# One pool of 4 KB slots, a rescaled rational step, and |h| added by an accumulating DMA

## The chip, the cores and the metric

The kernel runs on one core of a Trainium2 chip. The metric is the device time of one launch in microseconds (us). The core has TensorE (PE) for matmuls, VectorE (DVE), ScalarE (ACT) and GpSimd (POOL) for elementwise work, and SyncE (SP), which here only issues transfers (DMAs). All of them work in parallel and wait for each other through semaphores. Each of ACT, DVE, PE and POOL executes its own instructions strictly in the order in which the program was written out.

## The reference

Three layers over 12480 tokens of 128 channels, float32:

```python
a2k = softmax(scale * agents @ k.T); agent_v = a2k @ v            # 49 agents
x1  = softmax(scale * q @ agents.T) @ agent_v                     # (12480, 128)
h   = x1 @ w_in;   x2 = (h * sigmoid(h)) @ w_out                  # w_in (128, 2048)
h   = x2 @ w2_in                                                  # w2_in (128, 2048)
P   = a[0] + a[1]*h + a[2]*h**2 + a[3]*h**3
Q   = 1 + |b[0]|*|h| + |b[1]|*h**2
out = (P / (Q + 1e-06)) @ w2_out                                  # (12480, 128)
```

The four weight matrices come as float64 and go to the chip as their bits; the kernel turns them into float32 itself.

## The kernel before, in words

At the start SP queues 43 loads (`LOADS`: 13 of k, 13 of v, 16 pieces of 512 KB of the weights, the first of q). k is transposed on PE (step KT), scored against the agents (KS), exponentiated (EX), transposed back (ET) and multiplied with v (AV); the result goes into the weight of the first layer (F0 to F4, V0 to V2). A piece of the weights goes through C0 and C2 on DVE, C1 on ACT, C3 on POOL, and for w2_in C4 (ACT) and C5 (POOL) as well.

Then come 25 groups g of 512 tokens (the last has 192). For each group 8 pairs p of 128-wide hidden chunks run through these steps; h is a 128x1024 tile in PSUM, of which there are three slots:

- M1 (PE, L537 and L538): h of the first layer; S1 (ACT, L544): silu; M2 (PE, L551): the sum into one PSUM bank, x2. XS (DVE, L564 and L565) splits x2 into a high and a low part.
- M3 (PE, L574 to L576): h of the second layer. U (DVE L585 for four pairs, ACT L583 for the other four): a3*h + a2. W1 and W2 (DVE, L610, L614): two more Horner steps. AB (ACT, L592): |h|. N and Q (POOL, L598, L606): the denominator without its 1. An h slot is free again when AB and W2 have read it.
- L and R (ACT, L619, L622): Ln and then the sigmoid of its negative, which is the reciprocal of the denominator. They run over two pairs at a time (128x2048). Ln, sigmoid, silu and exp need different tables, so the Ln and sigmoid of a group come as a batch, with a table load (1.28 us) at each change.
- G2 (DVE, L626): the last Horner step times the reciprocal; M4 (PE, L635): the sum into one PSUM bank, ot. O1 (ACT, L647) copies it out, O2 (PE, L655) transposes it into the same bank, O3 (ACT, L661) copies that out, and SP stores it. The next group's M4 needs the bank back, that is O3.

Every second group a batch of q is transposed, scored and normalised (QT, QTc, QS, QV, QX, QM, QE, QN, QB, QBc, QBl) to give the input of M1 for two groups; QTc (L459) and QBc (L516) are ACT copies.

The order of all of this is not found at run time. `scheduled()` simulates the steps with the costs in `COST` and the numbers in `PLACE`, which set the preference of a step over others on its engine, and the program is written out in that order. Tiles in SBUF come from one ring for each kind: s 5, z 13, m 2, y 6 (8 KB each), and so on.

Of the kernel before, what the change touches and what calls it, by code (L numbers as in the profile page):

```python
# [100 lines left out]


def group_steps(groups, pairs, part=1.0):
# [60 lines left out]
    for job in range(16):  # L164
# [7 lines left out]
        split = job // 4 == 2  # L172
        after = [("C2", job, 0)] + [("KS", batches - 1, 0)] * (job >= 12)
        stage(3, after, [("w2", ("w2", job))] * split, [("cb", job)])
        if split:
            stage(4, [("C3", job, 0)], [], [("w2", job)])
            stage(5, [("C4", job, 0)], [], [("w2", job)])
    conv += [("V2", n, 0) for n in range(4)]
    for g in range(groups):
        b = g // 2  # L180
        for p in range(pairs):
            first = [("V2", p // 2, 0)] if g == 0 else []
            add("M1", g, p, [("QBl", b, 0)] + first, [("h", ("h1", g, p))], [("xt", b)])
            add("S1", g, p, [("M1", g, p)], [("s", ("s", g, p))], [("h1", g, p)])
            first = [("C3", 4 + p // 2, 0)] if g == 0 else []
            add("M2", g, p, [("S1", g, p)] + [("M2", g, p - 1)] * (p > 0) + first, [("x2", ("x2", g))] if p == 0 else [], [("x2", g), ("s", g, p)])
# [810 lines left out]
```

## Time and profile before

| | |
|---|---|
| median of 3 runs | 1265.34 us (1263.23 to 1265.42) |
| profiled execution, first to last instruction (span) | 1261.5 us |
| median run less that span | 3.8 us |
| busy share of the span | PE 98%, ACT 85%, DVE 80%, POOL 61% |
| mean granted clock of PE | 0.996 |

No separate time was recorded for the profiled execution, so its time is taken as its span and the 3.8 us around it. Busy time of PE is the union of its matmuls, whose ends are modelled; a gap between two matmuls is a real wait. The rows say what ended the idle time before an instruction, in square brackets.

### The profile page before, as it was taken

To read this page: it belongs to the slowest core of one execution; us is meant where nothing else is said; L and a number is where in the kernel's file an instruction comes from. 1 tells how busy PE (TensorE), PEld (TensorE's weight loads), DVE (VectorE), ACT (ScalarE), POOL (GpSimd) and SP (SyncE) were. 2 spreads that over 40 slices of the span, in tenths; PEclk is the share of its full clock that TensorE was granted. 3 is DMA by queue.
4 is the path that set the end of the run, shared out by engine and by line. 5 is a ranking of instruction groups with operands and counts; after the bars stand their busy time and mean duration, and the time that the engine had idled before them with its cause. 6 is when DMAs were issued, how large, how long until landed. Compare 5 with 4: busy or idle time off the path is not lost.

```text
span 1261.5 us, 12078 instructions
## 1 busy us (share of the span) xinstructions
PE 1235.0 (98%) x4393; PEld 740.7 (59%) x4393; DVE 1003.4 (80%) x960; ACT 1076.0 (85%) x997; POOL 764.2 (61%) x434
## 2 busy tenths in 40 slices
PE   9899899999999999999999999999999999999987
PEld 5656465556556556556566565565555565555654
DVE  4977887888868869869869869769769769769895
ACT  7677988988988988988988978978978979978896
POOL 2248667666566656656655755755755755755863
PEclk9999999999999999999999999999999999999999
DMA  9820000000000000000000000000000000000000
GB/s 343 303 78 1 1 17 9 8 17 9 9 17 9 8 18 9 9 17 9 9 17 9 9 17 9 9 17 9 1 25 9 1 12 9 1 8 9 9 1 20
DMA packets 14675, 34.75 MB, mean 28 GB/s; under 512 B 1575, under 2 KB 5720, under 8 KB 14616
## 3 DMA queue, kind: packets, MB, share of 16 engines
q1 hardware_dynamic: 14616, 33.98, 7.4%
q8 instruction: 35, 0.57, 0.2%
q14 instruction: 24, 0.20, 0.0%
HBM read 27.59 MB, written 6.39 MB: 27 GB/s over the span
## 4 chain that ended last, share of the span: by engine, by line
PE 86%; DVE 6%; ACT 4%; DMA 2%; issue 1%; POOL 0%; SPq 0%; POOLq 0%; ACTq 0%; DVEq 0%
PE x L551 25%; PE ot L635 23%; PE h L537 7%; PE h L574 7%; PE h L538 7%; PE h L576 7%; PE h L575 7%; DVE z L610 2%; DVE z L614 1%; DVE z L585 1%; PE h L468 1%; PE h L451 1%; DMA kv<-in_k_dram 1%; PE ot L655 1%; DVE z L626 1%
## 5 line engine op out<-in xcount | busy, mean ns | idle before, releaser
L598 POOL TENSOR_SCALAR y<-m,bab 128x1024 f32<-128x1024 f32 (+1 forms) x200 | 265.4, 1329 | 409.8 <-ACT m L592 402.9
L606 POOL TENSOR_TENSOR y<-y,m 128x1024 f32<-128x1024 f32 (+1 forms) x200 | 469.0, 2357 | 7.5
L551 PE MATMUL x<-s,wo 128*128 128x512 f32 (+1 forms) x800 | 358.9, 584 | 3.1 <-ACT s L544 2.8
L635 PE MATMUL ot<-z,w2o 128*128 128x512 f32 x768 | 349.8, 596 | 6.8 <-DVE z L626 4.6
L610 DVE TENSOR_TENSOR z<-z,h 128x1024 f32<-128x1024 f32 (+1 forms) x200 | 237.8, 1191 | 141.2 <-ACT z L583 134.1
L626 DVE SCALAR_TENSOR_TENSOR z<-z,a_sb,y 128x1024 f32<-128x1024 f32 (+1 forms) x200 | 264.6, 1372 | 4.7 <-ACT y L622 4.7
L592 ACT ACTIVATE m<-h 128x1024 f32<-128x1024 f32 (+1 forms) x200 | 197.1, 1000 | 81.2 <-PE h L576 72.9
L614 DVE SCALAR_TENSOR_TENSOR z<-z,a_sb,h 128x1024 f32<-128x1024 f32 (+1 forms) x200 | 249.9, 1252 | 5.0 <-ACT m L592 0.5
L544 ACT ACTIVATE s<-h 128x1024 f32<-128x1024 f32 (+1 forms) x200 | 193.3, 1005 | 59.5 <-PE h L538 59.1
L635 PEld LDWEIGHTS ot<-z,w2o 128*128 128x128 f32 x768 | 143.6, 190 | 162.2 <-issue 145.1
L551 PEld LDWEIGHTS x<-s,wo 128*128 128x128 f32 x800 | 147.7, 190 | 138.5 <-issue 127.0
L574 PE MATMUL h<-xh,w2l 128*128 128x512 f32 (+1 forms) x400 | 190.9, 477 | 1.6 <-DVE z L614 1.2
L619 ACT ACTIVATE y<-y,eps 128x2048 f32<-128x2048 f32 (+1 forms) x100 | 191.4, 1957 | 0.8 <-POOL y L606 0.5
L537 PE MATMUL h<-xt,w1a 128*128 128x512 f32 (+1 forms) x400 | 185.9, 466 | 0.8 <-DVE z L614 0.7
L622 ACT ACTIVATE y<-y 128x2048 f32<-128x2048 f32 (+1 forms) x100 | 185.0, 1878 | 0.3
L576 PE MATMUL h<-xh,w2h 128*128 128x512 f32 (+1 forms) x400 | 155.9, 390 | 0.0
L575 PE MATMUL h<-xl,w2h 128*128 128x512 f32 (+1 forms) x400 | 155.3, 388 | 0.0
L538 PE MATMUL h<-xt,w1b 128*128 128x512 f32 (+1 forms) x400 | 155.1, 389 | 0.0
L585 DVE TENSOR_SCALAR z<-h,a_sb 128x1024 f32<-128x1024 f32 (+1 forms) x100 | 130.8, 1312 | 5.7 <-PE h L576 3.8
L583 ACT ACTIVATE z<-h,a_sb 128x1024 f32<-128x1024 f32 (+1 forms) x100 | 118.3, 1184 | 5.5 <-PE ot L635 3.5
L537 PEld LDWEIGHTS h<-xt,w1a 128*128 128x128 f32 x400 | 75.6, 189 | 44.1 <-issue 16.0
L574 PEld LDWEIGHTS h<-xh,w2l 128*128 128x128 f32 x400 | 75.9, 190 | 36.7 <-issue 20.0
(108 smaller groups left out, 855.1 us busy)
## 6 DMA issues: line engine op xcount, KB each, us to landing
q<-in_q_dram SPq DMA_DIRECT2D x12, 512.0 KB, 3.3
out_dram<-ob SPq DMA_DIRECT2D x24, 256.0 KB, 2.0
raw<-in_moe_w_in_dram SPq DMA_DIRECT2D x8, 512.0 KB, 4.9
raw<-in_moe_w_out_dram SPq DMA_DIRECT2D x8, 512.0 KB, 7.5
s<-in_k_dram SPq DMA_DIRECT2D x7, 512.0 KB, 7.4
kv<-in_v_dram SPq DMA_DIRECT2D x7, 512.0 KB, 7.7
kv<-in_k_dram SPq DMA_DIRECT2D x5, 512.0 KB, 10.3
s<-in_v_dram SPq DMA_DIRECT2D x5, 512.0 KB, 8.0
```

The lines of the kernel that those rows point to most:

```text
L537: nc.tensor.matmul(h[:, c, :w], w1a[:, f], xt, start=True, stop=False)
L538: nc.tensor.matmul(h[:, c, :w], w1b[:, f], xt, start=False, stop=True)
L551: nc.tensor.matmul(x2_t[i][:, : cols(i)], wo[:, 2 * p + c, :], s[:, c, : cols(i)], start=(p == 0 and c == 0), stop=(p == NP - 1 and c == 1),)
L574: nc.tensor.matmul(h[:, c, :w], w2l[:, f], xh_t[i], start=True, stop=False)
L575: nc.tensor.matmul(h[:, c, :w], w2h[:, f], xl_t[i], start=False, stop=False)
L576: nc.tensor.matmul(h[:, c, :w], w2h[:, f], xh_t[i], start=False, stop=True)
L598: nc.gpsimd.tensor_scalar(out=y_t[i, p // 2][:, p % 2], in0=m_t[i, p], scalar1=bab[:, 1:2], scalar2=bab[:, 0:1], op0=ALU.mult, op1=ALU.add,)
L606: eng.tensor_mul(out=y, in0=y, in1=m_t.pop((i, p)))
L610: nc.vector.tensor_mul(out=z, in0=z, in1=h)
L614: nc.vector.scalar_tensor_tensor(out=z, in0=z, scalar=a_sb[:, 1:2], in1=h, op0=ALU.add, op1=ALU.mult)
L626: nc.vector.scalar_tensor_tensor(out=z, in0=z, scalar=a_sb[:, 0:1], in1=r, op0=ALU.add, op1=ALU.mult)
L635: nc.tensor.matmul(ot_t[i][:, : cols(i)], w2o[:, 2 * p + c, :], z[:, c, :], start=(p == 0 and c == 0), stop=(p == NP - 1 and c == 1),)
```

## The change

- Tiles of the groups no longer come from a ring for each kind. `NF = 35` slots of 4 KB (tag `f0` to `f34`) serve s, xh and xl, z, m, y, o, q and qT alike; a step takes the slot that the planner finds free first. 20 of them lie in memory that holds k, v, raw weights and conversion tiles at the start. Before, z, m and y lay in a pool that was opened when the whole start was over.
- x2 is scaled by B0 = |b[0]| in XS (now tensor_scalar and scalar_tensor_tensor on DVE). With h' = |b[0]|*h the denominator is 1 + |h'| + kap*h'^2, with one coefficient.
- SQ (ACT, new): y = (ROOT*h')^2 = kap*h'^2, in one ACT instruction of each pair. W1 becomes y + COEF[2]*h' (DVE, scalar_tensor_tensor), and U is gone.
- Y (new): |h'| is added onto y by a DMA that POOL issues (`accum_op=ALU.add`), 512 KB of m into 512 KB of y for each pair. N and Q on POOL are gone.
- L and R run on one pair (128x1024) at a time, and a batch starts when all 8 pairs' adds are planned as done (`READY_Y = 8`).
- O1, O3, QTc and QBc go from ACT to DVE (`COPY = 'DDDD'`); O1 also multiplies by LAST.
- CF (new): 33 DVE instructions on a 128x1 column or two and 2 on ACT work out the new coefficients once, after V2.
- `LOADS` is in another order, and nearly all of `PLACE` has other numbers. `SPLIT` is empty, so the steps SH and SL and the split M2 in the diff are never made; M1 to M4 and O2 are the matmuls they were.

```diff
-LOADS = "kk0kkkkk1kkkvkk2q4kvvvvvv><vvv56vv37?v;=:98"
+LOADS = 'kk51kkkkk20kkkvkk43vkqvvvvvv8v;?vv6vv9>7<=:'
...
-READY_Y = 4
+READY_Y = 8
...
+    add("CF", 0, 0, [("V2", 3, 0)], at=-3 + PLACE["CF"][0])
...
+            add("AB", g, p, after + then("AB", g, p), [("f", m)], [h, m], cost=ABS_COST[ABS[p]])
+            if POLY[p] == "S":
+                add("SQ", g, p, after, take_y, [h, y], cost=POLY_COST[POLY[p]])
+                add("W1", g, p, [("SQ", g, p)], [("f", z)], [h, z, y])
+                add("Y", g, p, [("W1", g, p), ("AB", g, p)], [], [m, y], cost=MAG_COST[MAG[p]])
...
+    def t_f(slot, dtype=F32, shape=None):
+        pool = work if slot < NKV + NRAW + NCA + NCB else late
+        return pool.tile(shape or [P, 2, GW], dtype, tag=f"f{slot}", name=f"f{slot}", bufs=1)
...
-        nc.vector.tensor_copy(xh, ps[:, :w])
-        nc.vector.tensor_sub(out=xl, in0=ps[:, :w], in1=xh.bitcast(F32))
+        nc.vector.tensor_scalar_mul(out=xh, in0=ps[:, :w], scalar1=B0)
+        nc.vector.scalar_tensor_tensor(
+            out=xl, in0=ps[:, :w], scalar=B0, in1=xh.bitcast(F32), op0=ALU.mult, op1=ALU.subtract
+        )
...
+    def SQ(i, p, slot):
+        y = part_of(y_t, i, p, slot)
+        nc.scalar.activation(y, h2_t[i, p][:, :, : cols(i)], AF.Square, scale=ROOT)
...
+            nc.vector.scalar_tensor_tensor(
+                out=part_of(z_t, i, p, slot), in0=h, scalar=COEF[2], in1=y_t[i, p],
+                op0=ALU.mult, op1=ALU.add,
+            )
...
-            out=y_t[i, p // 2][:, p % 2], in0=m_t[i, p],
-            scalar1=bab[:, 1:2], scalar2=bab[:, 0:1], op0=ALU.mult, op1=ALU.add,
...
+        if MAG[p] == "G":
+            nc.gpsimd.dma_start(out=y, in_=m, accum_op=ALU.add)
...
-    def L(i, h):
-        nc.scalar.activation(y_t[i, h], y_t[i, h], AF.Ln, bias=eps)
+    def L(i, p):
+        nc.scalar.activation(y_t[i, p], y_t[i, p], AF.Ln, bias=eps)
...
-        nc.scalar.copy(o[:, : cols(i)], ot_t.pop(i)[:, : cols(i)])
+            nc.vector.tensor_scalar_mul(out=o[:, 0, : cols(i)], in0=ps, scalar1=LAST)
...
-        nc.scalar.copy(ob, os_t.pop((i, 2))[:n, :].rearrange("p (j c) -> p j c", c=C))
+        (nc.scalar.copy if COPY[3] == "A" else nc.vector.tensor_copy)(ob, ps)
```

Three places show what the new order does. The first is ACT where the first silu stands, at the start of group 0. Before (L929 is V1, L731 and L733 are C1, L544 is S1):

```order
L929 CAST w1a<-h 128x512 x2
L731 ACTIVATE sb<-ec 128x512
L733 ACTIVATE mf<-ma 128x512
L544 ACT_TABLE_LOAD
L544 ACTIVATE s<-h 128x1024 x3
```

And now, on the same engine at the same place (L1110 is V1, L994 and L1009 are CF's two instructions, L621 is S1):

```order
L1110 CAST w1a<-h 128x512
L994 ACTIVATE cf<-b_sb 128x2
L1009 ACTIVATE cf<-a_sb 128x4
L621 ACT_TABLE_LOAD
L621 ACTIVATE f_831<-h 128x1024
L621 ACTIVATE f_834<-h 128x1024
L621 ACTIVATE f_841<-h 128x1024
```

The first silu stands behind CF's second instruction, which writes a column that CF's first DVE instructions read, and so waits for them.

The second place is ACT in a group in the middle, where the Ln batch begins. Before, the Ln (L619) of two pairs each, with |h| (L592) and U (L583) between them:

```order
L592 ACTIVATE m<-h 128x1024 [waits PE_49,Activation_49,Pool_49]
L619 ACT_TABLE_LOAD
L619 ACTIVATE y<-y,eps 128x2048
L583 ACTIVATE z<-h,a_sb 128x1024 [waits DVE_49,PE_49]
L592 ACTIVATE m<-h 128x1024 [waits PE_49,Activation_49,Pool_49]
L619 ACTIVATE y<-y,eps 128x2048
```

And now (L711 is |h|, L687 is SQ, L742 is Ln, L550 is QV; the tile f_4351 is the y that the SQ ahead of the table load wrote, DMASW the semaphores of POOL's DMAs):

```order
L711 ACTIVATE f_4349<-h 128x1024 [waits DVE_49,PE_49]
L687 ACTIVATE f_4351<-h,cf 128x1024 [waits DMASW6_49,Activation_49]
L742 ACT_TABLE_LOAD
L742 ACTIVATE f_4159<-f_4159,eps 128x1024
L742 ACTIVATE f_4153<-f_4153,eps 128x1024
L742 ACTIVATE f_4226<-f_4226,eps 128x1024
L742 ACTIVATE f_4175<-f_4175,eps 128x1024
L550 COPY f_4366<-h 128x512 [waits DVE_49,PE_49,Activation_49]
L742 ACTIVATE f_4224<-f_4224,eps 128x1024 [waits DMASW3_49]
L742 ACTIVATE f_4278<-f_4278,eps 128x1024
L742 ACTIVATE f_4351<-f_4351,eps 128x1024 [waits DMASW7_49]
```

The group's last square is right ahead of the batch, and the seventh Ln waits for the DMA that adds onto its result. In the next group |h| of a pair stands in place of QV, one Ln further down, and the Ln that waits is the seventh again.

The third place is the end, where group 22's sum is copied out while group 24's M3 and group 23's sigmoids run. Before, on ACT (L622 sigmoid, L647 O1, L661 O3):

```order
L622 ACTIVATE y<-y 128x2048
L592 ACTIVATE m<-h 128x2x192 x2
L622 ACTIVATE y<-y 128x2048
L647 COPY oT<-ot 128x512
L583 ACTIVATE z<-h,a_sb 128x2x192
L622 ACTIVATE y<-y 128x2048
L661 COPY ob<-ot 128x512
L622 ACTIVATE y<-y 128x2048
```

And now the same copies on DVE (L737 W2, L774 O1, L749 G2, L787 O3):

```order
L737 SCALAR_TENSOR_TENSOR f_7312<-f_7312,cf,h 128x2x192
L737 SCALAR_TENSOR_TENSOR f_7305<-f_7305,cf,h 128x2x192
L774 TENSOR_SCALAR f_7319<-ot,cf 128x512
L749 SCALAR_TENSOR_TENSOR f_7159<-f_7159,cf,f_7121 128x1024
L787 COPY f_7319<-ot 128x512
L749 SCALAR_TENSOR_TENSOR f_7153<-f_7153,cf,f_7143 128x1024
```

O1 and O3 have moved from a queue with sigmoids of 2048 columns to one with Horner steps of 1024 and 384.

## Rows read from the trace of the kernel before


**Rows 1.** Windows: us, busy of each engine (instructions), granted clock, DMA share, GB/s.

```profile
0.00:30.00 30.00, 28.29 (x169) 17.95 (x169) 13.56 (x26) 21.43 (x31) 6.32 (x16) 1.00 0.91 342
...
170.00:1170.00 1000.00, 998.65 (x3292) 590.09 (x3291) 802.26 (x705) 873.88 (x754) 620.94 (x336) 1.00 0.03 11
```

**Rows 2.** Chain of waits: start, us, engine, line, two M4 stretches 14 groups apart.

```profile
416.79 6.87 PE ot L635 x16
...
1087.35 6.87 PE ot L635 x16
```

**Rows 3.** Waits of PE from 65 to 170: us in total, times, longest.

```profile
PE ot L635 <- DVE z L626: 3.2, 1, 3.2
PE x L551 <- ACT s L544: 2.8, 2, 1.9
```

**Rows 4.** The same from 1200 to the end.

```profile
PE ot L655 <- ACT oT L647: 2.2, 2, 1.8
PE ot L635 <- ACT ob L661: 2.2, 1, 2.2
PE ot L635 <- DVE z L626: 1.4, 1, 1.4
PE h L574 <- DVE z L614: 0.9, 2, 0.7
```

**Rows 5.** Timeline of PE: start, us, idle before and its releaser.

```profile
64.91 0.80 PE L537 MATMUL h<-xt,w1a 128*128 128x512 f32 x1
...
155.33 3.22 PE L551 MATMUL x<-s,wo 128*128 128x512 f32 x4 [1.91 <-ACT s L544]
...
1233.58 2.86 PE L635 MATMUL ot<-z,w2o 128*128 128x512 f32 x4 [2.19 <-ACT ob L661]
...
1257.33 0.62 PE L655 MATMUL ot<-ident,oT 128*48 128x128 f32 x4 [0.46 <-ACT oT L647]
```

**Rows 6.** Groups by line from 170 to 1170: count, busy us, mean ns, idle before.

```profile
L626 DVE SCALAR_TENSOR_TENSOR z<-z,a_sb,y 128x1024 f32<-128x1024 f32 x168 | 225.1, 1390 | 0.0
...
L614 DVE SCALAR_TENSOR_TENSOR z<-z,a_sb,h 128x1024 f32<-128x1024 f32 x168 | 214.4, 1278 | 3.9
L610 DVE TENSOR_TENSOR z<-z,h 128x1024 f32<-128x1024 f32 x167 | 203.2, 1218 | 125.8 <-ACT z L583 118.9 <-ACT m L592 5.9
L592 ACT ACTIVATE m<-h 128x1024 f32<-128x1024 f32 x168 | 169.1, 1021 | 70.8 <-PE h L576 63.8 <-DVE z L585 5.1 <-POOL y L606 1.4
L619 ACT ACTIVATE y<-y,eps 128x2048 f32<-128x2048 f32 x84 | 164.4, 2000 | 0.3
...
L585 DVE TENSOR_SCALAR z<-h,a_sb 128x1024 f32<-128x1024 f32 x84 | 112.2, 1339 | 3.6 <-PE h L576 2.7 <-ACT m L592 0.9
L583 ACT ACTIVATE z<-h,a_sb 128x1024 f32<-128x1024 f32 x83 | 100.0, 1205 | 0.4 <-PE ot L635 0.3
...
L619 ACT ACT_TABLE_LOAD x21 | 26.9, 1283 | 0.4
...
L564 DVE CAST xh<-x 128x512 fp32r<-128x512 f32 x21 | 14.5, 691 | 57.4 <-PE x L551 57.4
...
L661 ACT COPY ob<-ot 128x512 f32<-128x512 f32 x21 | 12.4, 592 | 0.3 <-PE ot L655 0.3
```

**Rows 7.** DMA issues of the page: count, KB each, median us to landing.

```profile
q<-in_q_dram SPq DMA_DIRECT2D x12, 512.0 KB, 3.3
out_dram<-ob SPq DMA_DIRECT2D x24, 256.0 KB, 2.0
```

**Rows 8.** Timeline of POOL: one instruction by itself, and one beside DVE's L626.

```profile
100.47 1.19 POOL L598 TENSOR_SCALAR y<-m,bab 128x1024 f32<-128x1024 f32 x1 [2.73 <-ACT m L592]
...
157.21 3.30 POOL L598 TENSOR_SCALAR y<-m,bab 128x1024 f32<-128x1024 f32 x1 [1.09 <-ACT m L592]
```

**Rows 9.** Timeline of SP ahead of the last v load.

```profile
48.18 5.97 SPq L703 DMA_DIRECT2D raw<-in_moe_w_out_dram  x2
```

**Rows 10.** Timeline of DVE, an instruction on one column.

```profile
35.10 0.15 DVE L859 TENSOR_TENSOR mx<-ot,mx 128x1 f32<-128x1 f32 x1
```

More of the change, by code (lines that the diff above doesn't have):

```diff
@@ L112, in add @@
             at += PLACE.get(name + ">", (0.0,))[0] * (g > groups - 3)
-        eng, c = cost or COST[name]
+        eng, c = cost or (COPY_COST[name][COPY[list(COPY_COST).index(name)]] if name in COPY_COST else COST[name])
         if name in BATCH and g == groups // 2:
@@ L182, in group_steps @@
             first = [("V2", p // 2, 0)] if g == 0 else []
[L183 to L186, printed above, removed]
-        add("XS", g, 0, [("M2", g, p) for p in range(pairs)], [("xh", ("xh", g))], [("x2", g)])
+            add("M1", g, p, [("QBl", b, 0)] + then("M1", g, p) + first + [("XS", g - 1, 0)] * (g > 0 and p > 2), [("h", ("h1", g, p))], [("xt", b)])
@@ L188, in group_steps @@
+            add("M2", g, p, [after] + [("M2", g, ORDER[at - 1])] * (at > 0) + first, x2, [("x2", g)] + uses, cost=cost)
+        add("XS", g, 0, [("M2", g, p) for p in range(pairs)] + [("CF", 0, 0)] * (g == 0), [("f", ("xh", g))], [("x2", g)])
         for p in range(pairs):
[L189 removed]
+            h, z, y = ("h2", g, p), ("z", g, p), ("y", g, p)
             first = [("C5", 8 + p // 2, 0)] if g == 0 else []
[L191 removed]
@@ L209, in group_steps @@
+        add("O1", g, 0, [("M4", g, p) for p in range(pairs)], [("f", ("o", g))], [("ot", g)])
+        add("O2", g, 0, [("O1", g, 0)], [("ot", ("o2", g))], [("o", g)])
+        add("O3", g, 0, [("O2", g, 0)], [], [("o2", g), ("o", g)])
+        add("OD", g, 0, [("O3", g, 0)], [], [("o", g)])
     for b in range(batches):
-        chain = ("QT", "QTc", "QS", "QV", "QX", "QM", "QE", "QN", "QB", "QBc", "QBl")
+        chain = ("LQ",) * (b > 0) + ("QT", "QTc", "QS", "QV", "QX", "QM", "QE", "QN", "QB", "QBc", "QBl")
@@ L221, in group_steps @@
             add(
-                name, b, 0, [(chain[i - 1], b, 0)] if i else [("M1", 2 * b - 2, 0)] if b else [land["q", 0]], [takes[name]] if name in takes else [],
+                name, b, 0, [(chain[i - 1], b, 0)] if i else [("M1", 2 * b - 2, 0)] if b else [land["q", 0]], [takes[name]] if name in takes and (b or name != "QTc") else [],
                 uses.get(name, []), at=(2 * b if b else -2) + PLACE[name][0],
@@ L241, in scheduled @@
     free = {tag: [0.0] * n for tag, n in bufs.items()}
+    free["f"] = [None] * NF
+    held_by = [(slots, set(steps), steps) for slots, steps in group_steps.freed]
     taken = {tag: 0 for tag in bufs}
@@ L270, in may_start @@
         name, g, p = k
+        kind = name + MAG[p] if name == "Y" else name
         eng, _, _, takes, _, _ = ops[k]
@@ L273, in may_start @@
         for tag, _ in takes:
-            held = free[tag] if tag == "h" else [free[tag][taken[tag] % bufs[tag]]]
+            held = free[tag] if tag in "hf" else [free[tag][taken[tag] % bufs[tag]]]
             open_ = [x for x in held if x is not None]
@@ L282, in may_start @@
                     return None
-                done = sum(all(("Q", g, 2 * h + i) in end for i in (0, 1)) for h in range(4))
+                done = sum((done_y(h), g, h) in end for h in range(8))
                 if batch is None and (p or done < READY_Y):
@@ L287, in may_start @@
                 return None
-        if name == "R" and n_ln.get(g, 0) < 4:
+        if name == "R" and n_ln.get(g, 0) < 8:
             return None
-        if name in SHARED:
-            for e, x in seen.get((SHARED[name], g, p), {}).items():
+        if kind in SHARED:
+            for e, x in seen.get((SHARED[kind], g, p), {}).items():
                 if e != eng:
                     t = max(t, x + TELL[e].get(eng, 0.1))
-        if name in PORT:
+        if kind in PORT and eng in port:
             t = max(t, port["POOL" if eng == "DVE" else "DVE"])
@@ L307, in scheduled @@
         name, g, p = k
+        kind = name + MAG[p] if name == "Y" else name
         eng, cost, _, takes, uses, _ = ops[k]
@@ L310, in scheduled @@
         idle[eng], end[k] = t + cost, t + cost + TAIL[eng]
-        if name in PORT:
+        if kind in PORT and eng in port:
             port[eng] = max(port[eng], t + cost)
-        if name in SHARED:
-            seen.setdefault((SHARED[name], g, p), {})[eng] = end[k]
+        if kind in SHARED:
+            seen.setdefault((SHARED[kind], g, p), {})[eng] = end[k]
         slot = None
         for tag, what in takes:
-            if tag == "h":
+            if tag in "hf":
                 i = slot = min(
-                    (i for i, x in enumerate(free["h"]) if x is not None), key=lambda i: free["h"][i]
+                    (i for i, x in enumerate(free[tag]) if x is not None), key=lambda i: free[tag][i]
                 )
@@ L336, in scheduled @@
                 n_sig[g] = n_sig.get(g, 0) + 1
-                batch = None if n_sig[g] == 4 else batch
+                batch = None if n_sig[g] == 8 else batch
+        for slots, left, steps in held_by:
+            if k in left:
+                left.remove(k)
+                if not left:
+                    for i in slots:
+                        free["f"][i] = max(end[x] for x in steps)
         out.append((name, g, p, slot))
@@ L952, in attention_silu_rational_kernel @@
     for name, g, p, slot in scheduled(NG, NP, REST / GW):
-        if late is None and name in ("AB", "U"):
+        if late is None and slot is not None and slot >= NKV + NRAW + NCA + NCB:
             pre.close()
```

380 lines of the change are left out of this document (257 added, 123 removed), and 69 rows, old and new, of tables (COST, PLACE).

## The prediction

> **What bounds the kernel now.** I read the windows first. From 170 to 1170 us PE is busy for 998.65 of 1000 us at the full granted clock, ACT for 873.88, DVE for 802.26 and POOL for 620.94 [rows 1]: the matmuls set the pace, and the other three fit under them. The chain of waits shows that pace: the same M4 stretch stands at 416.79 and, 14 groups later, at 1087.35 [rows 2], which is 670.56 / 14 = 47.9 us a group. As batches of q come every second group, a period is two groups, 95.8 us.
>
> The order shows the same matmuls as before, so the pace can't get shorter. What can be won is the loss of PE outside the steady stretch. The first M1 starts at 64.91 and the last O2 ends at 1257.33 + 0.62 = 1257.95 [rows 5], 1193.0 us later. 24 whole groups are 24 x 47.9 = 1149.6. Group 24 has 192 of 512 columns; its matmuls take somewhat more than that share, and I put it at 0.43 of a group, 20.6 us (an estimate). That leaves 1193.0 - 1149.6 - 20.6 = 22.8 us of loss. The waits of PE name two thirds of it: 3.2 + 2.8 = 6.0 us at the start [rows 3] and 2.2 + 2.2 + 1.4 + 0.9 = 6.7 us at the end [rows 4]. Behind two of them four M2 or M4 matmuls take 3.22 and 2.86 us [rows 5]; 128x512 matmuls of that kind stand with 6.87 / 16 = 0.43 us each in [rows 2], so 1.7 for four. Each of the two waits thus costs another 1.1 to 1.5 us in slower matmuls at once, and about 2 (an estimate) with those behind them. So about 8 us lie at the start and 8.5 at the end. Removing all of it gives 1249 at best.
>
> **The steady stretch, engine by engine.** Sums for 1000 us, by [rows 6] unless said.
>
> ACT loses the four U, 100.0 us, and the four copies: O3 is 12.4 by its row, and O1, QTc and QBc are taken like it, some 47 together. It gains a square of 1024 columns for each of 168 pairs. The trace has no square; the nearest rows are |h| with 1021 ns and U with 1205 ns, the same shape out of PSUM, so 171 to 202 us, and I take 186. L and R on halves cost nothing to 39 us: 2000 ns for 2048 columns is 1.0 us for 1024 without a fixed part, and |h| with its 1021 ns bounds the fixed part at little. So ACT stands at 873.9 - 100 - 47 + 186 + 20 = 933 (898 to 954), still below 998.65.
>
> DVE loses the other four U, 112.2, and gains the four copies. The nearest DVE row is XS with 691 ns for 512 columns: 42 x 0.69 = 29 for O1 and O3, some 27 for QTc and QBc. W1 becomes an instruction like W2, 1278 for 1218 ns, +10. G2 may keep its 1390 ns or fall to the 1278 of W2, 0 to -19. DVE: 802 - 112 + 56 + 10 - 10 = 746. CF is not in this stretch.
>
> POOL's 621 us go. In its place stands one issue for each pair; its engine is free for it.
>
> So no engine comes up to PE. I laid the printed order of one period end to end with these durations: PE stays without a gap, its h slots come free 0.6 to 1.7 us before they are wanted. I cost the steady stretch at 0, covered by these margins.
>
> **The new wait.** The seventh Ln waits for the add onto the last square of its group. Between the end of that square and this Ln stand a table load of 1.28, six Ln of 1.0 to 1.1 and one QV or |h| of 0.6 (as L661) to 1.0 us [rows 6], 7.9 to 8.9 us. W1, which reads y before the add, takes 1.28 us and a hop first, about 1.4. So 6.5 us are left for the issue and the transfer, and with 1.3 to 1.7 us of slack behind it (by the same laying out) a late add costs nothing up to about 8 us. The trace has no accumulating DMA. From below: a 512 KB load takes 3.3 us from issue to landing, 256 KB 2.0 [rows 7], so 1.3 us for 256 KB more. From above: the add reads its 512 KB of target as well, 2 x 1.3 more, 5.9 us. Issuing by software on POOL has no row; one SP issue lies below it. I take about 5 with the issue, nearer the lower end, for that row includes the read and the write of 512 KB. At 5 the seventh Ln waits for nothing. Queued behind a late Ln would be the eight sigmoids, the next silus (h slots, so M1) and through them G2 and M4.
>
> **The start.** The last v load moves from the 38th to the 37th place, with one piece fewer of the weights before it. Ahead of it SP stood 5.97 us for the raw slots of two weight pieces [rows 9], so up to that can be won. Against it the last k load has two pieces of 512 KB more ahead of it, 1 MB at 342 GB/s [rows 1], 3 us. As k's chain and v's both must end before the first M1, I take 0 (-3 to +2). CF is 33 instructions on a column at 0.15 us [rows 10], 5.0 us of DVE after V2, and the first silu waits for the first few of them, about 0.7. The rest lies beside M1 and M2 of group 0, before the first W1; if that cover is gone it costs 5. The waits of [rows 3] don't go: the first batch of Ln now needs all eight pairs, while the first M4 waits for G2 as before. I take +1 for the whole start (-3 to +6).
>
> **The end.** The two longest waits are for O1 and O3 on ACT [rows 4], each behind a sigmoid of 2048 columns (about as long as an Ln, 2.0 us [rows 6]). On DVE a copy now waits behind a Horner step of 1.28, and DVE has no U. Laid out with the row durations about 4 us of the 8.5 stay: O1, O2 and O3 still follow each other, and PE has little else to do by then. Gain 4.5 (-8 to +2).
>
> **The sum.** The profiled execution has a span of 1261.5 and 3.8 us around it, together the median of 1265.3. Start +1, steady 0, end -4.5: 1258.0 for the span, **1261.8** with what lies around it; I say 1262.
>
> **Rivals.** *The add comes late, on the seventh Ln of each group.* This ends on the other side. POOL has to write the transfer's list itself. A POOL instruction that takes 1.19 us by itself took 3.30 while DVE ran G2 [rows 8]: beside G2, which reads two tiles of SBUF, POOL was held for 2.1 us. The Trainium skill warns of just this kind of DMA (SBUF — State Buffer, 🎯 Summary: rules for kernel authors): one that POOL issues can starve for its descriptors beside some DVE instructions, and SP or ACT should issue it instead. The trace has no such DMA, and the page names DVE's two-port modes for it, not two SBUF inputs. In this kernel the price by rows is 5.9 + 0.4 + 2.1 = 8.4 us if POOL is held once and each byte of the target counts, and 10.5 if it is held twice. Beyond 8 us every group pays: 24 x 0.4 = 10 us, 24 x 2.5 = 60 us. 1270 to 1325. For it speaks that squares come every 6.0 us (47.9 / 8) and the add reads and writes 5.2 us worth of bytes by the slope; against it, that around the batch DVE has the last Horner steps, with one tile of SBUF and one of PSUM, and G2 comes after the sigmoids.
>
> *The start gets later.* CF's 5 us fall on the path, as the first Horner steps wait behind the weights' conversions on DVE, and the two k pieces' 3 us with it: +5 to +8 with the tail's gain halved, 1268 to 1273. For it: the first M4 already waits 3.2 us for DVE [rows 3]. Against it: M1 and M2 of group 0 fill PE for long before that M4.
>
> *Nothing to be seen.* The tail's gain is eaten by +3 to +5 at the start, or O1 and O3 wait behind Horner steps that themselves wait for h. 1263 to 1268.
>
> *More is won.* Without U and without POOL's 620.94 / 168 = 3.7 us for each pair [rows 1] the first group's G2 comes earlier and the 3.2 us wait goes too: -6 more, under 1256.
>
> **Chances.** The forecast 0.43, between 1256 and 1262.8; more won 0.07; nothing to be seen 0.22; a late add 0.16; a later start 0.12. A measurement of this kernel tells 0.2%, 2.5 us, from no change: faster under 1262.8, slower over 1267.9. Faster 0.50, same 0.22, slower 0.28. The range from 1253 to 1275 leaves out the upper part of the late add, some 0.13, and the lower part of the gain, 0.03. The forecast's own range is 1256 to 1263.
>
> **What would show it.** Right: the same M4 rows 14 groups apart stay at 670.6 us; the waits of PE in the steady stretch remain under 2 us; the seventh Ln has no idle before it from POOL's DMA; an add lands within 6.5 us of its issue; ACT is near 933 and DVE near 746 in 170 to 1170; the first M1 begins at 64 to 68; O2 and the next M4 wait for DVE under 2 us each at the end. Wrong: a period above 95.8 with ACT idle before Ln (the late add); the first silu or the first M4 some us later (the start); the waits of [rows 4] as long as before with DVE's name on them; ACT over 990, if a square costs far more than U.

## The result and the profile after

The changed kernel takes 1273.38 us (median of 4 runs, 1272.29 to 1274.15) against 1265.17 for the kernel before in the same comparison: 1.0069 times, interval 1.0055 to 1.0083. It is slower by 8.2 us, where a gain of 3 was forecast. The profiled execution has a span of 1270.5 us, 9.0 more than before, and a mean granted clock of 0.997.

The first view is the windows. This is the kernel before in the stretches around [rows 1], with the same columns:

```profile
60.00:90.00 30.00, 27.42 (x89) 15.91 (x90) 25.80 (x45) 23.06 (x33) 11.84 (x8) 1.00 0.25 77
90.00:120.00 30.00, 30.00 (x107) 18.38 (x106) 23.18 (x24) 19.02 (x22) 22.95 (x14) 1.00 0.03 12
120.00:170.00 50.00, 44.42 (x147) 27.17 (x147) 39.94 (x33) 43.67 (x37) 35.11 (x18) 0.97 0.00 1
1170.00:1220.00 50.00, 47.36 (x195) 31.76 (x194) 44.83 (x39) 45.29 (x42) 39.96 (x22) 1.00 0.02 6
1220.00:1261.50 41.50, 32.90 (x121) 19.39 (x119) 26.32 (x37) 29.67 (x34) 18.14 (x16) 0.96 0.04 15
```

And the changed kernel (busy PE, PEld, DVE, ACT, POOL, then clock, DMA share, GB/s):

```profile
60.00:90.00 30.00, 23.38 (x77) 14.20 (x77) 27.91 (x72) 19.56 (x28) 10.48 (x8) 0.94 0.28 88
90.00:120.00 30.00, 27.13 (x89) 14.76 (x87) 25.91 (x31) 19.71 (x24) 10.13 (x11) 1.00 0.51 108
120.00:170.00 50.00, 43.97 (x144) 25.76 (x145) 34.12 (x32) 46.64 (x48) 8.29 (x10) 0.97 0.54 103
170.00:1170.00 1000.00, 997.51 (x3285) 588.82 (x3285) 728.52 (x688) 926.95 (x934) 143.38 (x167) 1.00 0.50 99
1170.00:1220.00 50.00, 49.23 (x184) 31.02 (x183) 37.95 (x35) 44.15 (x49) 7.73 (x9) 1.00 0.53 105
1220.00:1270.50 50.50, 42.17 (x170) 25.66 (x168) 29.86 (x43) 37.22 (x54) 10.48 (x9) 0.99 0.33 55
```

Idle time of PE is what is left of each window. It grows by 4.0 us from 60 to 90 (2.6 to 6.6), by 2.9 from 90 to 120 (0 to 2.9), 0.5 from 120 to 170 and 1.1 in the 1000 us of the steady stretch. From 1170 to the end it falls by 2.1 (11.2 to 9.1). With 0.6 before 60 this is 6.9 of the 9.0 us; the other 2.1 are busy time of PE (1237.1 against 1235.0) for the same matmuls, which the mean granted clock (0.997 for 0.996) does not explain. So most of the loss lies between 60 and 120 us, in the first group.

The steady stretch keeps its pace. Two M4 stretches 14 groups apart in the chain of waits of the changed kernel, for [rows 2]:

```profile
487.04 6.87 PE ot L758 x16
...
1157.67 6.87 PE ot L758 x16
```

670.63 / 14 = 47.9 us a group, as before. Its groups by line from 170 to 1170, for [rows 6] (L701 is W1, L749 G2, L687 the square, L742 Ln, L728 the add's issue):

```profile
L701 DVE SCALAR_TENSOR_TENSOR f<-h,cf,f 128x1024 f32<-128x1024 f32 x168 | 213.3, 1280 | 169.4 <-ACT f L687 96.0 <-ACT f L711 71.7
L749 DVE SCALAR_TENSOR_TENSOR f<-f,cf,f 128x1024 f32<-128x1024 f32 x168 | 210.3, 1278 | 4.2 <-ACT f L745 4.0
L687 ACT ACTIVATE f<-h,cf 128x1024 f32<-128x1024 f32 x168 | 187.1, 1127 | 1.9 <-PE h L679 1.9
L742 ACT ACTIVATE f<-f,eps 128x1024 f32<-128x1024 f32 x168 | 180.1, 1138 | 0.4
...
L728 POOL DMA_DIRECT2D f<-f x167 | 143.4, 882 | 852.5 <-DVE f L701 736.8 <-issue 58.7 <-PE h L679 54.3
```

The page's row of the add, for [rows 7] (KB each, median us from issue to landing), and all that ACT waits for it in the steady stretch (us in total, times, longest), which is |h| and not Ln:

```profile
f<-f POOLq DMA_DIRECT2D x192, 512.0 KB, 5.0
```

```profile
ACT f L711 <- DMA f<-f: 1.4, 2, 1.1
```

The add is on time and hides: 1.4 us in 1000. In the batch at 510 the issue begins at 511.04, so by the median its add lands about 516.0, and the seventh Ln (third of the four that begin at 515.37) starts near 517.5: some 1.5 us to spare.

PE at the start and at the end (timeline), for [rows 5]:

```profile
66.80 0.79 PE L614 MATMUL h<-xt,w1a 128*128 128x512 f32 x1
...
74.03 3.00 PE L658 MATMUL x<-f,wof 128*128 128x512 f32 x4 [3.64 <-ACT f L621]
...
1218.80 8.74 PE L758 MATMUL ot<-f,w2o 128*128 128x512 f32 x20
...
1239.57 0.66 PE L780 MATMUL ot<-ident,f 128*128 128x128 f32 x4 [2.27 <-DVE f L774]
...
1266.03 0.62 PE L780 MATMUL ot<-ident,f 128*48 128x128 f32 x4 [0.51 <-DVE f L774]
```

M1 begins 1.9 us later than before, and the first M2 waits 3.6 us for the first silu. At the end O2 still waits, now with DVE's name; no M4 waits for O3 any more.

What holds the first silu back is CF. Its first and last DVE instructions in the timeline:

```profile
69.03 0.94 DVE L991 TENSOR_SCALAR cf<-cf 128x2 f32<-128x2 f32 x1
70.01 1.25 DVE L985 TENSOR_TENSOR cf<-cf 128x1 f32<-128x1 f32 x2
...
76.26 0.16 DVE L985 TENSOR_TENSOR cf<-a_sb,cf 128x1 f32<-128x1 f32 x1
```

CF holds DVE from 69.03 to 76.42, 7.4 us, where the prediction had 5.0. ACT stood 3.25 us ahead of CF's second instruction there, at 71.34, and the first silu came at 72.86.

### The profile page after: what moved, and what is told of

Its sections match the earlier page's. It is cut to its first block, busy times and chain, and to the rows that moved or that the text cites. A ratio compares the mean times of both kernels' runs of the same rounds, so it can differ in the third digit from the quotient of the medians.

```text
span 1270.5 us, 12342 instructions
## 1 busy us (share of the span) xinstructions
PE 1237.1 (97%) x4393; PEld 736.8 (58%) x4393; DVE 926.3 (73%) x981; ACT 1135.3 (89%) x1210; POOL 204.5 (16%) x234
## 4 chain that ended last, share of the span: by engine, by line
PE 63%; ACT 4%; DVE 1%; issue 0%; DMA 0%; POOL 0%; ACTq 0%; POOLq 0%
PE ot L758 18%; PE x L658 18%; PE h L677 5%; PE h L679 5%; PE h L614 5%; PE h L678 5%; PE h L615 5%; ACT f L745 1%; PE ot L780 1%; ACT f L687 1%; ACT f L742 1%; ACT f L711 1%; PE h L544 1%; PE h L530 1%; DMA f<-f 0%
## 5 line engine op out<-in xcount | busy, mean ns | idle before, releaser
L701 DVE SCALAR_TENSOR_TENSOR f<-h,cf,f 128x1024 f32<-128x1024 f32 (+1 forms) x200 | 248.3, 1254 | 190.6 <-ACT f L687 101.8
L658 PE MATMUL x<-f,wof 128*128 128x512 f32 (+1 forms) x800 | 356.4, 585 | 3.8 <-ACT f L621 3.8
L758 PE MATMUL ot<-f,w2o 128*128 128x512 f32 x768 | 351.1, 595 | 1.2 <-DVE f L787 0.8
L728 POOL DMA_DIRECT2D f<-f x200 | 174.6, 903 | 970.4 <-DVE f L701 811.5
L749 DVE SCALAR_TENSOR_TENSOR f<-f,cf,f 128x1024 f32<-128x1024 f32 (+1 forms) x200 | 244.9, 1252 | 11.4 <-ACT f L745 10.9
L737 DVE SCALAR_TENSOR_TENSOR f<-f,cf,h 128x1024 f32<-128x1024 f32 (+1 forms) x200 | 245.6, 1249 | 1.6 <-ACT f L711 0.3
L711 ACT ACTIVATE f<-h 128x1024 f32<-128x1024 f32 (+1 forms) x200 | 201.8, 1010 | 44.2 <-PE h L679 41.3
L687 ACT ACTIVATE f<-h,cf 128x1024 f32<-128x1024 f32 (+1 forms) x200 | 217.7, 1103 | 10.6 <-PE h L679 10.0
L621 ACT ACTIVATE f<-h 128x1024 f32<-128x1024 f32 (+1 forms) x200 | 185.5, 1010 | 32.7 <-PE h L615 20.3
L742 ACT ACTIVATE f<-f,eps 128x1024 f32<-128x1024 f32 (+1 forms) x200 | 210.0, 1116 | 1.6 <-DMA f<-f 1.2
L677 PE MATMUL h<-f,w2l 128*128 128x512 f32 (+1 forms) x400 | 199.4, 498 | 3.8 <-ACT f L711 2.5
L678 PE MATMUL h<-f,w2h 128*128 128x512 f32 (+1 forms) x400 | 155.0, 387 | 0.6 <-DVE f L666 0.6
L679 PE MATMUL h<-f,w2h 128*128 128x512 f32 (+1 forms) x400 | 155.3, 388 | 0.0
L615 PEld LDWEIGHTS h<-xt,w1b 128*128 128x128 f32 x400 | 75.6, 189 | 24.1 <-issue 10.7
```

The costliest lines, as they stand in the source:

```text
L615: nc.tensor.matmul(h[:, c, :w], w1b[:, f], xt, start=False, stop=True)
L658: nc.tensor.matmul(x2, wof[:, at : at + P], s_t[i, p][:, c, :w], start=start, stop=stop)
L677: nc.tensor.matmul(h[:, c, :w], w2l[:, f], xh_t[i], start=True, stop=False)
L678: nc.tensor.matmul(h[:, c, :w], w2h[:, f], xl_t[i], start=False, stop=False)
L679: nc.tensor.matmul(h[:, c, :w], w2h[:, f], xh_t[i], start=False, stop=True)
L687: nc.scalar.activation(y, h2_t[i, p][:, :, : cols(i)], AF.Square, scale=ROOT)
```

## The experiments

The theory after the result: CF on DVE, between the weights' conversions, is what the start loses. Rivals were that ACT's wait inside CF is the cost, that the copies moved to DVE are, and that the add is late or nearly so.

**The add, made dearer in three ways.** First the add done by POOL itself, with no DMA:

```diff
-            nc.gpsimd.dma_start(out=y, in_=m, accum_op=ALU.add)
+            nc.gpsimd.tensor_add(out=y, in0=y, in1=m)
```

> The changed kernel with the add done by POOL itself instead of a DMA that POOL issues, in the same order; about 2.4 us of POOL for each pair as L606 before, and landed 2 to 3 us sooner. If the accumulating DMA cost nothing, the time stays within 2 us of the changed kernel's, and G2 on DVE goes back to 1.39 us. If the DMAs hold something up, it gets faster by more than 2.

1297.35 us, 1.0253 [1.0239, 1.0267]. Its groups by line from 170 to 1170:

```profile
L749 DVE SCALAR_TENSOR_TENSOR f<-f,cf,f 128x1024 f32<-128x1024 f32 x164 | 244.4, 1515 | 4.1 <-ACT f L745 4.0
...
L728 POOL TENSOR_TENSOR f<-f,f 128x1024 f32<-128x1024 f32 x163 | 442.3, 2728 | 553.5 <-DVE f L701 544.6 <-issue 8.1 <-ACT f L711 0.3
```

G2 takes 1515 ns beside it for 1278 with the DMA, and PE falls from 997.51 to 986.51 busy: the DMA pays for itself.

Then the DMA twice, which also changes the result (|h| counts twice):

```diff
             nc.gpsimd.dma_start(out=y, in_=m, accum_op=ALU.add)
+            nc.gpsimd.dma_start(out=y, in_=m, accum_op=ALU.add)
```

> The changed kernel with every accumulating DMA issued twice, one after the other, so that the add lands some 5 us later (its result has |h| twice). In the trace of the changed kernel an add lands 5.0 us after its issue, about 1.5 us before the seventh Ln wants it. By the prediction's sum a late add costs every group what is beyond some 8 us from W1: 10.9 against 8 gives 2 to 3.5 us for each of 24 groups, 50 to 85 us in all. If ACT's 70 idle us in 1000 take it up, under 10.

1987.15 us, 1.570 [1.5678, 1.5721]. Waits of the whole execution:

```profile
POOL f L729 <- DMA f<-f: 1065.1, 197, 8.1
ACT f L621 <- DMA f<-f: 246.5, 55, 9.4
```

POOL waits for the first DMA before it issues the second one, so pairs of them follow each other on one queue and POOL becomes the bound. This says nothing about how late one add may be; it was the wrong experiment for that.

So the delay was put into POOL's queue, a read of z (which W1 writes, so that it can't start early) and three memsets ahead of each issue:

```diff
+            nc.gpsimd.tensor_copy(out=scrap[:, 0:1], in_=z_t[i, p][:, 0, 0:1])
+            for _ in range(3):
+                nc.gpsimd.memset(scrap, 0.0)
             nc.gpsimd.dma_start(out=y, in_=m, accum_op=ALU.add)
```

> The changed kernel with POOL held for about 3 us between W1 and the issue of each accumulating DMA (a copy of one column of W1's result and three memsets of a scrap tile that nothing reads), so that every add lands 3 us later. The trace of the changed kernel leaves 1.5 us before the seventh Ln wants its add. If the prediction's sum holds (no cost up to about 8 us from W1 to landing, then all of it in every group), the Ln waits 1.5 us in each group and the time is 10 to 36 us more. If ACT's idle time takes it up, under 5.

1536.05 us, 1.214 [1.2123, 1.2157]; (1536.05 - 1273.38) / 24 = 10.9 us a group. Waits from 170 to 1170, some 17 groups (L688 the square, L712 |h|, L746 Ln, L741 W2):

```profile
ACT f L688 <- DMA f<-f: 40.1, 21, 3.5
ACT f L712 <- DMA f<-f: 31.3, 14, 3.7
ACT f L746 <- DMA f<-f: 26.7, 16, 3.6
...
DVE f L741 <- POOL scrap L729: 89.3, 52, 4.4
```

Ln waits 26.7 / 17 = 1.6 us a group. ACT waits more elsewhere: the square and |h| wait (40.1 + 31.3) / 17 = 4.2 us for slots whose add is still under way, as a slot of m comes free only when the DMA has landed. The 5.2 us a group of W2 belong to the read of z that the experiment brought in, and PE waits above all for them, here over the whole execution:

```profile
PE h L678 <- DVE f L741: 113.2, 50, 4.6
PE h L615 <- DVE f L741: 39.2, 23, 3.6
```

That is some 6 us for each of 24 groups. So this run shows that a late add makes the square and |h| wait for slots, besides Ln; it does not give the price of a late add, as most of its 10.9 us can be the experiment's own. The changed kernel's ACT has 1.4 us of such waits in the steady stretch.

**Copies.** O1 and O3 back on ACT in all groups (`nc.scalar.activation(..., AF.Copy, scale=LAST)` and `nc.scalar.copy`):

> The changed kernel with O1 and O3 back on ACT, at the same places of the order. The prediction's term for the end said that these two on DVE save 4.5 us: then this is 3 to 5 us slower than the changed kernel, with waits of 2 us for O1 and O3 at the end. If what saved time at the end was the other changes (halved sigmoids, no U), within 1 us of it; the steady stretch stays at 95.8 us for two groups either way, as ACT has 70 us of 1000 idle.

1304.18 us, 1.0308 [1.0292, 1.0323]. The largest of its waits of PE, over the whole execution:

```profile
PE ot L758 <- ACT f L787: 13.9, 10, 1.7
```

PE falls to 980.52 busy from 170 to 1170. The order was planned with these copies on DVE; on ACT O3 comes late ten times in 25 groups. The reverse, the same two copies on DVE in the kernel before:

> The kernel before with O1 and O3 on DVE, at the same places of its order. The prediction's term for the end said that these two on DVE save 4.5 us; the changed kernel's trace shows 2 less loss at the end. If the move alone did that, this is 2 to 4 us faster than before, with the steady stretch unchanged. If O1 and O3 there stand behind Horner steps that wait for h, the M4 behind them comes late in each group, and it is 5 to 30 us slower, as O1 and O3 put back on ACT made the changed kernel 31 us slower.

1279.69 us, 1.0121 [1.0108, 1.0135], PE 992.78 busy of 1000 for 998.65. In either order the other engine is the worse one, so neither run prices the end by itself.

That was done with `or i >= NG - 3` on the engine's choice, so that only the last three groups change; first in the kernel before (to DVE), then in the changed one (to ACT):

> The kernel before with O1 and O3 on DVE in the last three groups alone, at the same places. The prediction's term for the end (each waits behind a sigmoid of 2048 columns on ACT) says up to 4.5 us faster; 1 to 3 us if half of the wait is the round trip of O1, O2 and O3 itself. Not faster if DVE's queue there holds the copies as long as ACT's.

> The changed kernel with O1 and O3 on ACT in the last three groups alone, at the same places. The prediction's term for the end says 4.5 us slower. By the profile after, the end lost 2 us less than before: then 1 to 3 us slower. Under 1 us if the order of the end is what gained.

1267.32 us, 1.0018 [1.0009, 1.0027], and 1276.24, 1.0091 [1.0078, 1.0105]: each worse than its own base, by some 2 and 3 us. Waits of PE from 1170 to 1280 in the first of them:

```profile
PE ot L656 <- DVE oT L648: 2.6, 2, 2.1
PE ot L635 <- DVE ob L663: 2.5, 1, 2.5
```

These are the waits for O1 and O3 of [rows 4], 2.2 and 2.2 us on ACT, now 2.6 and 2.5 on DVE. In the changed kernel PE waits 4.0 us for O1 on DVE from 1180 to the end, and 4.4 for it on ACT; for O3 it waits on neither. In neither order does the other engine shorten these waits.

This pair also shows how fine such a reading can be. The same M3 near the end starts at 1205.57 in the kernel before; in this variant:

```profile
1208.67 0.47 PE L574 MATMUL h<-xh,w2l 128*128 128x512 f32 x1 [0.69 <-DVE z L614]
```

3.1 us later, though no instruction ahead of it was changed. The granted clock was 0.77 there for 0.89 from 30 to 45 us, and 0.89 for 1.00 from 60 to 75. In the other variant, too, the first XS, ahead of anything that was changed, stands at 102.60 for 100.10 in the changed kernel, with a granted clock of 0.82 for 0.89 from 75 to 90 and 0.84 for 0.99 from 60 to 75. Differences of 2 to 3 us between programs can come with the start's clock, so these two times do not price the end, and only the waits speak.

QBc of the first batch on ACT (`or b == 0` on its engine's choice), as it lies on the way to the first M1:

> The changed kernel with the two copies QBc of the first batch of q on ACT instead of DVE; they stand between the division F2 and the copy F4 on DVE, 1.4 us, while ACT is idle there. Theory (they delay V0 and so the first M1): the first M1 1 to 1.4 us earlier and the time 1 to 1.5 us less. Rival (PE's round trip to DVE hides them, or the start has another bound): within 0.5 us.

1272.98 us, 1.0061 [1.0049, 1.0073]; the intervals of this and of the changed kernel overlap, nothing to be seen.

**CF, moved and left out.** CF right behind the first X2, early in the queue:

```diff
+    plan.remove(cf_step)
+    plan.insert(1 + next(i for i, x in enumerate(plan) if x[:3] == ('X2', 0, 0)), cf_step)
```

> The changed kernel with the step CF (33 DVE and 2 ACT instructions) written out behind X2, when the loads are still running, in place of behind V2; nothing else moves. Theory (the loss is at the start: the first silu waits on ACT for CF, 3.25 us, PE then waits 3.64 us for it and comes back at the lower clock): the first silu 3 to 4 us earlier, PE's wait before the first M2 from 3.64 to under 1 us, the time 4 to 6 us less than the changed kernel's, about 1268. Rival (the start is set by the conversions of the weights and by the Horner steps on DVE further down, so that CF's place only shifts where PE waits): under 1.5 us less.

1274.34 us, 1.0071 [1.0058, 1.0085]: no gain. CF runs from 38.71 to 44.2 on DVE, and PE meets the delay earlier:

```profile
69.37 2.81 PE L1107 MATMUL h<-wi,avT 128*128 128x512 f32 x6 [1.33 <-DVE avT L1102]
```

This V0 began at 62.78 in the changed kernel: 6.6 us later for some 5.5 us of CF. Then ACT's wait alone, its second instruction moved up behind its first, so that the first silu waits for nothing of DVE:

```diff
+        nc.scalar.activation(aa, a_sb, AF.Abs)
         one_(least, ab, ALU.mult, 1e-12, ALU.add, 1e-15)
...
-        nc.scalar.activation(aa, a_sb, AF.Abs)
```

> The changed kernel with CF in its place, but its second ACT instruction ahead of the first DVE instruction and into columns of its own, so that ACT waits for nothing in CF; DVE has the same 33 instructions at the same place. If ACT's wait is what costs, the time falls as much as with CF early, 3.5 to 5 us. If the 7 us of DVE are what costs (conversions and Horner steps behind them), it stays within 1 us of the changed kernel.

1273.26 us, 1.0063 [1.0050, 1.0076]: nothing. Timeline of PE:

```profile
70.87 1.96 PE L658 MATMUL x<-f,wof 128*128 128x512 f32 x4 [0.28 <-ACT f L621]
...
79.77 0.50 PE L614 MATMUL h<-xt,w1a 128*128 128x512 f32 x1 [2.52 <-ACT f L621]
```

The wait of the first M2 is gone (0.28 for 3.64), and one of 2.5 us stands at a later M1. My theory that ACT's wait in CF was the cost falls; DVE's time is left. CF as the first step of all, with its two small loads first in ACT's queue:

```diff
+    nc.scalar.dma_start(out=a_sb, in_=ca.partition_broadcast(P))
+    nc.scalar.dma_start(out=b_sb, in_=cb.partition_broadcast(P))
...
+    plan.insert(0, cf_step)
```

> The changed kernel with a and b loaded first of all, from ACT's queue, and CF written out ahead of every other step, where DVE has nothing to do yet; the other steps keep their order. CF early had put CF's DVE instructions between the softmax steps, which made the first M1 6.6 us later; here they stand ahead of all of them. Theory (CF between V2 and the first silu, 7.3 us of DVE and 3.3 of ACT, is what the order had not allowed for): the first M1 stays at 66.8, the first XS comes 5 us earlier than 100.1, and the time falls by 4 to 6 us, to about 1268. Rival (the start is set by the Horner steps and the first Ln batch from 100 us on): XS earlier but the time within 2 us of the changed kernel's.

1277.14 us, 1.0091 [1.0076, 1.0106], the worst of the three places. Timeline of ACT:

```profile
12.51 0.20 ACT L993 ACTIVATE cf<-b_sb 128x2 f32<-128x2 f32 x1 [6.50 <-DMA b_sb<-in_moe_b_dram]
```

Everything of k on ACT is queued behind this 6.5 us wait for the load. Then the test from the other side, CF alone added to the kernel before, behind V2, where nothing reads its results:

```diff
+        if after_v2:
+            CF(0)
+        after_v2 = (name, g) == ("V2", 3)
```

> The kernel before with CF's 35 instructions added behind V2, where the changed kernel has them; their results aren't used. Theory: ACT and DVE are held there by the same 3 and 7 us, so it is 3 to 6 us slower than before, 1268 to 1271. Rival (the start of before has room for it): under 1.5 us slower.

1272.41 us, 1.0051 [1.0039, 1.0064]: a span of 1268.1, 6.6 us more than before. CF is 5.6 us of DVE there (66.93 to 72.5), and its ACT instructions wait 0.55. Waits from 60 to 90, of ACT and of PE:

```profile
ACT w2h L763 <- POOL w L759: 5.6, 1, 5.6
```

```profile
PE h L540 <- ACT s L547: 4.2, 1, 4.2
PE x L554 <- ACT s L547: 1.8, 1, 1.8
```

The path can be read off: behind CF on DVE stand the C2 of two weight pieces, POOL's C3 waits for them, ACT's C4 for C3, and silus stand behind C4 in ACT's queue, which PE waits for. Then the changed kernel with CF left out (its body empty, the coefficients set to 0.5, so that the output is another):

> The changed kernel without CF's 35 instructions; its column of coefficients is filled with one number instead, which leaves the computation of the coefficients out, and everything else stays as it was. With CF added the kernel before got 7 us slower. Theory: CF costs the changed kernel as much, 5 to 8 us, so this takes 1266 to 1268, with the first XS 5 to 6 us earlier than 100.1. Rival (the changed kernel's start has another bound besides, for instance the Horner steps and squares of group 0, which take the gain up again as with the second ACT instruction moved): under 2 us.

1269.21 us, 1.0028 [1.0018, 1.0039]: 4.2 us of the 8.2 come back. Its first M1 starts at 69.45, 2.7 us later than in the changed kernel (66.80), so 4.2 need not be all that CF costs. And CF whole, but on POOL, behind the fourth C3, with powers for reciprocals and the root:

```diff
-            nc.vector.tensor_tensor(out=out, in0=in0, in1=in1, op=op)
+            nc.gpsimd.tensor_tensor(out=out, in0=in0, in1=in1, op=op)
...
-        nc.vector.reciprocal(out=inv, in_=B0)
+        two(inv, B0, ALU.pow, minus)
...
+    fourth = [i for i, x in enumerate(plan) if x[0] == "C3"][3]
+    plan.insert(fourth + 1, cf_step)
```

> The changed kernel with the coefficients worked out by POOL, behind its fourth C3, where POOL has nothing to do for 9.9 us; 40 instructions on a column or so, reciprocals and the root by its power operation. DVE and ACT have nothing of CF. If POOL's room is enough, it comes as near to the kernel without CF as 1 us. If POOL's instructions take more than 10 us together, the conversions behind them (C3) come late and 2 to 6 us of it are lost again.

1267.94 us, 1.0020 [1.0011, 1.0029]. This is the best version with the change in it: 5.4 us, 0.4%, under the changed kernel, and 0.2% behind the kernel before. Its first and last instruction on POOL:

```profile
25.08 0.58 POOL L994 TENSOR_SCALAR cf<-b_sb 128x1 f32<-128x1 f32 x2 [0.19 <-DMA b_sb<-in_moe_b_dram]
...
37.23 0.19 POOL L988 TENSOR_TENSOR cf<-a_sb,cf 128x1 f32<-128x1 f32 x1
```

12.3 us there, where POOL has room and DVE and ACT have nothing of CF: the C3 behind it begins at 37.37, for 35.36 in the changed kernel. Windows:

```profile
60.00:90.00 30.00, 27.19 (x91) 15.74 (x91) 22.33 (x39) 21.30 (x30) 13.71 (x9) 0.94 0.33 106
90.00:120.00 30.00, 26.19 (x86) 14.98 (x85) 28.35 (x32) 20.25 (x22) 10.16 (x10) 1.00 0.58 118
```

PE's idle time from 60 to 90 is 2.8, that of the kernel before (2.6). What stays is the next window: 3.8 us idle where the kernel before has none. With QBc of the first batch on ACT besides:

> The same with the two copies of the first batch of q on ACT. Alone that made 0.4 us at most. If they were hidden behind CF there, they now come through, 1 us less than with CF on POOL; else the same.

1268.22 us, 1.0023 [1.0013, 1.0032], the same.

**The rest, from 90 to 120.** In this window DVE is busy for 28.35 of 30 us. W2 of group 0 was left out on top of CF on POOL (so its polynomial is cut short, `if i == 0: return`); then its squares too, a memset on POOL in their place:

> The kernel with the coefficients on POOL, without the Horner step W2 in group 0 (the output of group 0 lacks it). In the changed kernel and in this one PE loses 2.9 us between 90 and 120 us, where the eight M3 of group 0 stand nearly in a row and wait for the h slots that W1 and W2 give back, 2.5 us a pair on DVE against 1.4 on PE. If this loss goes through to the end, it is 1.5 to 3 us faster than with W2 in group 0. If ACT's squares and |h| (2.1 us a pair) or the first Ln batch hold the same slots anyway, under 1 us.

> As the kernel without W2 in group 0, and the eight squares of group 0 are left out as well: POOL fills their tiles with a number, so that ACT has |h| alone there (the output of group 0 is not the reference's). Without W2 alone the waits of PE moved from DVE to ACT and PE stood at 135.88 us where it stood with W2. If ACT's 8 us of squares in group 0 hold the first silus of group 1 and the first Ln, PE is 2 to 4 us ahead at that place and the time is 2 to 3 us less, at the level of the kernel before. If not, what is left of the loss at the start is not in group 0's second layer.

1268.67 us, 1.0031 [1.0019, 1.0044], and 1269.83, 1.0041 [1.0029, 1.0053]: nothing comes back. In the first, DVE falls to 19.13 in the window, yet PE still stands 3.9 us there, and the next transposes of q's scores (QX, L560), here in its timeline, begin to the hundredth where they begin with CF on POOL alone:

```profile
113.33 0.51 PE L617 MATMUL h<-xt,w1a 128*128 128x512 f32 x1 [1.14 <-DVE f L704]
...
116.26 3.57 PE L661 MATMUL x<-f,wof 128*128 128x512 f32 x4 [1.72 <-ACT f L624]
...
135.88 0.66 PE L560 MATMUL h<-ident,f 128*128 128x128 f32 x4 [0.26 <-ACT f L553]
```

One wait goes, and W1 (L704) and the silu take its place. But the clock takes part, too. The M2 at 116.26 is 1.6 us ahead of its place with CF on POOL alone (1.1 of them were there at the first XS), and its four matmuls take 3.57 us where they take 1.98 there:

```profile
117.84 1.98 PE L661 MATMUL x<-f,wof 128*128 128x512 f32 x4
```

The windows around it, first with CF on POOL alone, then without W2 as well, have a granted clock of 1.00 and 0.89:

```profile
105.00:120.00 15.00, 12.28 (x43) 7.39 (x42) 13.89 (x12) 11.72 (x12) 5.62 (x7) 1.00 1.05 196
105.00:120.00 15.00, 12.14 (x38) 7.37 (x38) 5.86 (x5) 11.11 (x11) 4.51 (x6) 0.89 1.05 196
```

With the squares gone the way from the first XS to the second is 37.8 us for 40.8, but the third XS stands at 183.07 for 182.42: given back, with a granted clock of 0.91 from 150 to 170, 1.00 with CF on POOL alone. What sets this window is not settled, and these two runs do not clear W2 and the squares, as matmuls at the lower clock level took back at least part of what PE was ahead.

**Another order.** At last the planner was given other numbers in `PLACE`, chosen by its own forecast, with CF on POOL and the first QBc on ACT:

> The kernel with the coefficients on POOL and the first QBc on ACT, its order written out anew: the planner is told that CF costs DVE and ACT nothing, and the numbers that set the preferences are other ones, with which its own simulated end comes 1.9 us sooner than that of the order of the changed kernel. If the start's order is what is left of the loss against the kernel before (2.8 us with the coefficients on POOL), this takes 1265 to 1267. If the rest lies in what no order moves (eight squares and eight |h| on ACT ahead of the first Ln), it stays at 1268.

1272.07 us, 1.0055 [1.0042, 1.0069]. From 60 to 170 PE is idle for 9.7 us, for 10.7 with the same two moves in the old order, but in the steady stretch it falls from 996.88 busy to 992.95: what the start gained is lost there.

## Why the prediction was wrong

*The steady stretch at 0: right.* 47.9 us a group; PE's idle time there rose by 1.1 us in 1000. ACT 927 for a forecast of 933, DVE 729 for 746; the square took 1127 ns (1021 to 1205 had been the bounds, the sum went by 186 us and got 187.1), G2 fell to 1278.

*The add at about 5 us, Ln not waiting: right.* It lands after 5.0 us (median; 4.5 to 8.2), and in the steady stretch Ln waits for none. The rival of a late add, at 0.16, did not occur. POOL's issues take 882 ns on the mean, also with DVE's Horner steps and G2 beside them, and none is held for 2 us. The Trainium skill (SBUF — State Buffer, 🎯 Summary: rules for kernel authors) warns that such a DMA starves beside some DVE instructions; this case doesn't show it with the instructions DVE runs here. But the prediction counted Ln alone, and the slots wait for the landing too: the square and |h| 4.2 us a group when POOL's issue was put off.

*The start at +1: this step failed.* By the windows PE's idle time up to 170 us rose by 8.0 (0.6, 4.0, 2.9 and 0.5). M1 came 1.9 us later, which the bounds for the loads allowed (-3 to +2); CF was the miss. The prediction had CF as 5.0 us whose rest "lies beside M1 and M2 of group 0, before the first W1". That cover is not there. It looked at who reads CF's results, not at who stands behind CF in DVE's queue: the conversions of the weights, which POOL, ACT and, through the silus, PE wait for. DVE had no room, with 25.80 us busy of 30 from 60 to 90 in the kernel before. CF alone in that kernel cost 6.6 us of span; CF left out of the changed one gave 4.2 back, CF on POOL 5.4. Its duration was off as well, 7.4 us for 5.0. The rival "the start gets later", 1268 to 1273 at 0.12, comes nearest: it puts CF's time on the path by way of the weights' conversions, but with the first Horner steps waiting behind them, where the runs show C3, C4 and the silus. The median lies 0.4 us above it.

*The end at -4.5: mis-sized.* By the windows it is -2.1, and not for the reason given: in the two end runs the waits for O1 and O3 are as long on DVE as on ACT. The end's order is another: 20 M4 stand in one piece at 1218.80, while in the kernel before M4 wait 2.2 us for O3 and 1.4 for G2 [rows 4]. That this is the gain is argued, not shown.

So of the 8.2 us between the medians 4.2 to 5.4 are CF on DVE (left out, or on POOL), and PE stands still for another 3 to 4 between 90 and 120, partly set off at the end. Their cause is open: W2 and the squares of group 0 were removed and the time did not move, but the clock fell where PE was ahead, and the whole is near what the clock makes between two programs.

## What to carry to other kernels

A one-off setup of tiny instructions can cost about its whole length (6.6 us for 5.6 in the kernel before) when it stands in a queue that the rest of the start waits behind: ask what is queued behind it, not only who reads its results, and give it to an engine with idle time there, even at twice its duration. Work that is off the critical path in the steady stretch, such as the copies, sets times in a fixed order, so moving it to another engine needs a new order. A DMA that adds onto a tile can hide well, as here, but it holds both of its tiles until it has landed, so count the wait for slots besides that of the reader. And an experiment that takes work away may show nothing because the matmuls behind a gap run at the lower clock: read the granted clock of the stretch beside it.
